# A matmul queue that no longer waits on its own semaphore, one moved matmul pair and a reordered load queue in a fused attention and gMLP kernel

## The chip, the cores and the metric

The kernel runs on one core of a Trainium2 chip. The metric is device time of one launch in microseconds (us). Traces come from one profiled execution; the times beside them come from separate runs.

## What is computed

The input x is 2048 x 512 in bf16. It is layer-normalised once; two branches read the result, and the output is x plus both. Cut to what matters:

```python
xn = _layernorm(x, axis=-1)
return x + _A_ref(xn, A_wqkv, A_wo) + _B_ref(xn, B_w_in, B_w_sp, B_b_sp, B_w_out)

# _A_ref: H = 32 heads of Dh = 16, each position looks at W = 8 positions, dil = 2 apart
logits = jnp.einsum('bhsd,bhswd->bhsw', q, kg) * scale    # masked where the position is < 0
o = jnp.einsum('bhsw,bhswd->bhsd', _softmax(logits), vg)  # then @ wo

# _B_ref: Fh = 896
z = _gelu(jnp.einsum('bsd,df->bsf', x, w_in))
z1, z2 = z[..., :Fh], _layernorm(z[..., Fh:], axis=-1)
g = jnp.einsum('ts,bsf->btf', w_sp, z2) + b_sp[None, :, None]
return jnp.einsum('bsf,fd->bsd', z1 * g, w_out)
```

## The kernel before

The 2048 positions are cut into 16 blocks of 128 rows, and these into four groups of four. Everything is a list of named tasks; each belongs to one engine, and knows what it reads and writes. `schedule` puts the tasks of each engine in order by estimated times, but `plan.orders` (lines 1037 to 1101) gives long hand-written orders that it must keep. `emit` (line 222) then writes each engine's tasks with the semaphore waits that their dependencies need. Each engine has one semaphore, which every task that isn't a DMA raises by one at its end (`sem_pe` for TensorE); each DMA channel has its own.

In `emit`, a task that depends on an earlier task of the same engine waits for that engine's own semaphore too, unless the engine is already known to have passed it (lines 260 to 277). On TensorE this concerns two tasks that write to the same PSUM bank with nothing of another engine between them.

The names that matter, with their lines:

- `ldx0` to `ldx15` (L543): loads of x blocks, 128 KB each. `ldw_in2a_0`, `ldw_in2b_1` and so on (L553): halves of the z2 part of w_in. `ldq`, `ldk` (L565) and `ldwv` (L573): the q, k and v weights, 512 KB each. SyncE issues most of these; ScalarE's queue issues three of the first ones.
- `bnst`, `bnag` (L610, L613), `rstd` on POOL (L615) and `norm` (L624): the layer norm of one block; `ctr` (L619) is the centring of block 0 alone.
- `xTr0b`, `xTr1a` (L640): transposing a half of a block on TensorE against the identity, two 128x128 matmuls each. `xTe0b`, `xTe1a` (L646): ScalarE's copy of it to SBUF. Only blocks 0 to 3 go this way; `xTd0` and `xTd4` to `xTd15` (L628) are transposes by DMA, issued by SyncE. Block 0 has both: TensorE's copy feeds its z2, `xTd0` feeds the rest.
- `z2_1_0a` (L802): for block 1, output half 0 (448 of the 896 columns) and contraction half a: two 128x448 matmuls. Halves a and b of one output add up in one PSUM bank. For block 0 half b comes first. `z2g1_0` (L813): ScalarE's gelu of it, with the sum along the row. `z2s` (L835): the sum of squares.
- `Q0_0`, `K0_0` (L678): q and k for the first group of four blocks, four 128x512 matmuls each. Q0_0 needs the four transposed blocks and `ldq`, K0_0 also `ldk`. `QKe` (L686) copies them out. `V0` (L660) likewise, with `Ve` (L664).
- `prod`, `padd` (L702, L707), `dd`, `sm`, `sz`, `srec`, `sattn` (L727 to L779): DVE's products, sums and softmax.
- `z1` (L825, gelu at L830), then `g0_0` and so on (L935): the product with w_sp, 16 matmuls a task. ScalarE first writes the bias into the bank (`gs`, L929), TensorE adds, and DVE multiplies with z1 (`u`, L942), which frees the bank.
- `out` (L1001, L1005): both output projections into one bank; `fin` (L1014) copies it, `st` (L1017) stores. `OTd` (L973) are the DMA transposes of the attention result that `out` reads.

Before the first loads have landed, TensorE runs eight `warm` matmuls (L582), and one more, `fill0`, between its first transposes and the first z2 half.

TensorE's order begins warm, xTr0b, xTr0a, fill0, z2_0_0b, z2_0_1b, xTr1a, xTr1b, z2_0_0a, z2_0_1a, z2_1_0a, z2_1_0b, z2_1_1a, xTr2a, xTr2b, z2_1_1b, z2_2_0a, z2_2_0b, xTr3a, xTr3b, z2_2_1a, z2_2_1b, z2_3_0a, z2_3_0b, z2_3_1a, z2_3_1b, Q0_0, K0_0. All later TensorE work follows in a fixed order as well: Q, K, V and z2 by groups, z1, g, out.

In the built program ten TensorE tasks wait on `sem_pe`: fill0, z2_0_0a, z2_0_1a, z2_1_0b, z2_1_1b, z2_2_0b, z2_2_1b, z2_3_0b, z2_3_1b and z2_4_0.

Of the kernel before, what the change touches and what calls it, by code (L numbers as in the profile page):

```python
# [14 lines left out]
class Plan:  # L15
# [79 lines left out]
    def schedule(self, lookahead=1000, slack=120.0, dma_bw=300.0, xbar_bw=190.0,  # L95
# [21 lines left out]
        def lat(d, t):  # L117
            if d.dma is not None:
                return 150.0
            if d.eng == t.eng:  # L120
                return 35.0
            return 210.0 if d.eng == "pe" else 80.0

        cur_tbl = [None]
# [10 lines left out]
        while remaining:  # L135
            best = None
            for e in ENGS:
# [6 lines left out]
                for t in pl:  # L144
                    ok = all(p.start is not None for p in before.get(t, ()))
                    ready = 0.0
                    for d in t.deps:
                        if d.end is None:
                            ok = False
                            break  # L150
                        r = d.end + lat(d, t)
                        if r > ready:
                            ready = r
                    if ok:
                        st_ = max(eng_free[e], ready + t.margin)
                        if t.tbl is not None and t.tbl != cur_tbl[0] and cur_tbl[0] is not None:
                            st_ += sw_bias
                        cands.append((st_, t))
# [24 lines left out]
            st, t = best  # L183
            e = t.eng
# [37 lines left out]
    def emit(self, nc, block, sems, chan_sems):  # L222
        cnt = {e: 0 for e in ENGS}
        ccnt = {}
        for e in ENGS:
            for t in self.order[e]:
                if t.dma is None:
                    cnt[e] += 1
                    t.count = cnt[e]
                    t.tok = (("E", e), t.count)  # L230
        for t in self.tasks:
            if t.dma is not None:
                c = t.dma["chan"]
                ccnt[c] = ccnt.get(c, 0) + 16
                t.count = ccnt[c]
                t.tok = (("C", c), t.count)
        self.chan_totals = dict(ccnt)
        for t in sorted(self.tasks, key=lambda x: (x.start, x.idx)):
            ck = {}
            for d in t.deps:  # L240
                for k, v in d.clock.items():
                    if ck.get(k, 0) < v:
                        ck[k] = v
            ck[t.tok[0]] = max(ck.get(t.tok[0], 0), t.tok[1])
            t.clock = ck

        engines = {"pe": nc.tensor, "act": nc.scalar, "dve": nc.vector, "pool": nc.gpsimd, "sp": nc.sync}
        starters = {"pe": block.tensor, "act": block.scalar, "dve": block.vector, "pool": block.gpsimd,
                    "sp": block.sync}
        self.n_waits = 0  # L250

        def semof(key):
            return sems[key[1]] if key[0] == "E" else chan_sems[key[1]]

        def run_engine(e):
            def body(eng):
                known = {}
                for t in self.order[e]:
                    need = {}
                    dl = [d for d in t.deps if known.get(d.tok[0], 0) < d.tok[1]]  # L260
                    for d in dl:
                        k, v = d.tok
                        implied = False
                        for d2 in dl:
                            if d2 is d:
                                continue
                            c2 = d2.clock.get(k, 0)
                            if c2 > v or (c2 == v and d2.tok != d.tok):
                                implied = True
                                break  # L270
                        if implied:
                            continue
                        if need.get(k, 0) < v:
                            need[k] = v
                    for k, v in need.items():
                        eng.wait_ge(semof(k), v)
                        self.n_waits += 1
                    for d in t.deps:
                        for k, v in d.clock.items():
                            if known.get(k, 0) < v:  # L280
                                known[k] = v
                    last = t.fn(eng)
                    assert last is not None, "task %s returned no instruction" % t.name
                    if t.dma is None:
                        last.then_inc(sems[e], 1)
                    else:
                        last.then_inc(chan_sems[t.dma["chan"]], 16)
                self._final_hook(e, eng)
            starters[e](body)

        for e in ENGS:
            run_engine(e)
# [21 lines left out]
    warm=8,  # L314
    fill0=1,
# [4 lines left out]
def build_kernel(nc, A_x, A_wqkv, A_wo, B_x, B_w_in, B_w_sp, B_b_sp, B_w_out, out, report=False, sched_kw=None,  # L320
# [79 lines left out]
    with ExitStack() as es:  # L400
# [633 lines left out]
        for q in qord:  # L1034
# [8 lines left out]
                z2g1_1  # L1043
            """.split(),
            """
                ldx0 ldx1 ldw_in2a_0 ldw_in2b_0 ldx3 ldx4 ldq xTd0 ldx5 ldk ldx6 ldx7 ldwv
            """.split(),
            """
                warm xTr0b xTr0a fill0 z2_0_0b z2_0_1b xTr1a xTr1b z2_0_0a z2_0_1a z2_1_0a z2_1_0b z2_1_1a xTr2a xTr2b
                z2_1_1b z2_2_0a z2_2_0b xTr3a xTr3b z2_2_1a z2_2_1b z2_3_0a z2_3_0b z2_3_1a z2_3_1b Q0_0 K0_0 Q0_1 K0_1  # L1050
                Q0_2 K0_2 Q0_3 K0_3 V0 V1 V2 V3 V4 V5 V6 V7 Q1_0 K1_0 Q1_1 K1_1 Q1_2 K1_2 Q1_3 K1_3 z2_4_0 z2_4_1 z2_5_0
                z2_5_1 z2_6_0 z2_6_1 z2_7_0 z2_7_1 V8 V9 V10 V11 Q2_0 K2_0 Q2_1 K2_1 Q2_2 K2_2 Q2_3 K2_3 z2_8_0 z2_8_1
# [28 lines left out]
                zm0_2 zm2 zq2 sm1_0 sm2_0 sm3_0 ssub0 prod1_2 prod1_3 padd1_1 ze2 zv2 padd1_2 zn8 zn9 zn10 zn11 prod2_0  # L1081
                prod2_1 zm0_3 zm3 zq3 padd2_0 dd0_1 dd1_1 sm1_1 sm2_1 sm3_1 ssub1 ze3 zv3 prod2_2 zn12 zn13 zn14 zn15
                prod2_3 padd2_1 padd2_2 prod3_0 prod3_1 padd3_0 u0_0 prod3_2 u1_0 sz1_0 sz2_0 sz3_0 srec0 sattn0 u2_0
                sz1_1 sz2_1 sz3_1 srec1 sattn1 u3_0 dd0_2 dd1_2 u4_0 sm1_2 sm2_2 sm3_2 ssub2 prod3_3 u5_0 sz1_2 sz2_2
                sz3_2 srec2 u6_0 sattn2 padd3_1 u0_1 padd3_2 u1_1 pv0_0_0 pv0_0_1 u2_1 pva2048_0_0 u3_1 pva1024_0_0
                pvc0_0 u4_1 pv0_1_0 u5_1 dd0_3 dd1_3 sm1_3 u6_1 sm2_3 sm3_3 ssub3 pv0_1_1 u0_2 sz1_3 sz2_3 sz3_3 srec3
                u1_2 sattn3 pva2048_0_1 pva1024_0_1 pvc0_1 pv1_0_0 pv1_0_1 u2_2 pva2048_1_0 u3_2 pva1024_1_0 pvc1_0 u4_2
                pv1_1_0 u5_2 pv1_1_1 pva2048_1_1 pva1024_1_1 pvc1_1 pv2_0_0 u6_2 pv2_0_1 pva2048_2_0 pva1024_2_0 pvc2_0
# [32 lines left out]
def bass_parallel_sum__sliding_local_dilated__mixer_gmlp__prompt_kernel(  # L1121
    nc, A_x, A_wqkv, A_wo, B_x, B_w_in, B_w_sp, B_b_sp, B_w_out, out
):
    build_kernel(nc, A_x, A_wqkv, A_wo, B_x, B_w_in, B_w_sp, B_b_sp, B_w_out, out)
# [28 lines left out]
```

## Time and profile before

| what | value |
|---|---|
| three runs | 237.16 us median, 236.94 to 238.07 |
| the profiled execution | 237.23 us, span 235.1 us |
| TensorE matmuls (PE) | 230.5 us busy, 98% of the span, 1103 instructions |
| VectorE (DVE) | 202.4 us, 86% |
| ScalarE (ACT) | 118.5 us, 50% |
| GpSimd (POOL) | 51.5 us, 22% |
| granted TensorE clock | 1.000 |
| DMA | 41.88 MB, mean 178 GB/s |

The span runs from the first to the last instruction in the trace; the execution's own time is 2.1 us longer. Busy shares are means over stages with different limits, so they don't say what a local change is worth. Matmuls overlap: a 128x448 matmul lasts 352 ns, but in a stream the next one starts 189 ns after it (32 of them in 6.05 us), so a busy TensorE need not be at its pace. PEld is the load of the stationary operand, which goes on beside the matmuls.

### The profile page before, as it was taken

The page shows a single profiled execution, that of the slowest core. Times are in us where ns is not written, and L with a number is a line of the kernel's source. Part 1 is how long each engine was busy: PE and PEld are TensorE (multiplying, and loading weights), DVE is VectorE, ACT ScalarE, POOL GpSimd, SP SyncE. Part 2 cuts the span into 40 slices and gives each one's busy share as a digit, 9 for nine tenths or more (in the row PEclk, how much of TensorE's full clock was granted, in tenths as well). Part 3 has the DMA queues.
Part 4 walks back from the last instruction along what each step waited for, and adds up shares of the span by engine and source line. Part 5 has one row for each costly group of instructions (what it writes and reads, how often), then busy time and mean ns, then how long its engine had stood idle before and what let it go on. Part 6 is the DMA issues. An engine that isn't in the chain of part 4 may idle for free.

```text
span 235.1 us, 2969 instructions
## 1 busy us (share of the span) xinstructions
PE 230.5 (98%) x1103; PEld 109.8 (47%) x1103; DVE 202.4 (86%) x231; ACT 118.5 (50%) x233; POOL 51.5 (22%) x67
## 2 busy tenths in 40 slices
PE   7899999999999999999999999999999999999996
PEld 2344455455454444444444444444444444444454
DVE  4579869998998989997999994999999999999600
ACT  3698578988988987954012125232223432201442
POOL 4437982862591050001201000010000000000000
PEclk9999999999999999999999999999999999999999
DMA  7997670299919799591529999999746788602232
GB/s 230 237 297 140 154 185 16 80 192 283 382 74 174 163 247 284 111 251 46 161 62 256 191 255 256 245 186 354 217 122 174 187 240 216 189 3 45 72 84 67
DMA packets 87709, 41.88 MB, mean 178 GB/s; under 512 B 66816, under 2 KB 86544, under 8 KB 87696
## 3 DMA queue, kind: packets, MB, share of 16 engines
q1 hardware_dynamic: 71616, 23.37, 47.9%
q10 hardware_dynamic: 14640, 14.13, 19.6%
q0 software_dynamic: 1440, 4.21, 6.1%
q8 instruction: 8, 0.13, 0.2%
q14 instruction: 5, 0.04, 0.1%
HBM read 20.05 MB, written 5.26 MB: 108 GB/s over the span
## 4 chain that ended last, share of the span: by engine, by line
PE 96%; DVE 1%; DMA 1%; issue 0%; POOL 0%; ACT 0%
PE ps L935 41%; PE ps L678 12%; PE ps L802 10%; PE ps L1005 10%; PE ps L825 10%; PE ps L1001 6%; PE ps L660 6%; DMA arena<-in_A_x_dram 1%; DVE fpool L610 1%; PE ps L640 0%; POOL fpool L615 0%; DVE arena L619 0%; DVE arena L624 0%; DVE fpool L613 0%; ACT arena L1014 0%
## 5 line engine op out<-in xcount | busy, mean ns | idle before, releaser
L935 PE MATMUL ps<-arena 128*128 128x512 bf16 x448 | 97.5, 379 | 0.0
L935 PEld LDWEIGHTS ps<-arena 128*128 128x128 bf16 x448 | 43.8, 98 | 52.8
L929 ACT ACTIVATE ps<-arena 128x512 f32<-128x512 bf16 x28 | 16.5, 599 | 58.5 <-DVE arena L942 58.4
L960 DVE TENSOR_TENSOR arena<-arena 128x4096 bf16<-128x4096 bf16 x16 | 36.3, 2284 | 0.4
L702 DVE TENSOR_TENSOR arena<-arena 128x4096 bf16<-128x4096 bf16 x16 | 36.1, 2281 | 0.1
L678 PE MATMUL ps<-arena 128*128 128x512 bf16 x128 | 28.3, 379 | 0.0
L964 DVE TENSOR_TENSOR arena<-arena 128x4096 bf16<-128x4096 bf16 (+1 forms) x16 | 28.0, 1752 | 0.3
L707 DVE TENSOR_TENSOR arena<-arena 128x4096 bf16<-128x4096 bf16 x12 | 27.4, 2287 | 0.2
L1005 PE MATMUL ps<-arena 128*128 128x512 bf16 (+2 forms) x126 | 27.1, 355 | 0.0
L802 PE MATMUL ps<-arena 128*128 128x448 bf16 x128 | 26.4, 353 | 0.8 <-ACT arena L646 0.3
L825 PE MATMUL ps<-arena 128*128 128x512 bf16 x112 | 24.3, 379 | 0.0
L678 PEld LDWEIGHTS ps<-arena 128*128 128x128 bf16 x128 | 14.5, 113 | 13.1
L1014 ACT ACTIVATE arena<-ps 128x512 bf16<-128x512 f32 (+2 forms) x17 | 9.5, 557 | 20.0 <-PE ps L1005 18.6
L942 DVE TENSOR_TENSOR arena<-ps,arena 128x512 bf16<-128x512 f32 x28 | 19.0, 679 | 0.0
L1005 PEld LDWEIGHTS ps<-arena 128*128 128x128 bf16 x126 | 13.5, 113 | 11.0
L802 PEld LDWEIGHTS ps<-arena 128*128 128x128 bf16 x128 | 11.8, 98 | 13.6 <-PE ps L802 1.5
L686 ACT ACTIVATE arena<-ps 128x1024 bf16<-128x1024 f32 x16 | 16.3, 1019 | 2.8 <-PE ps L678 2.2
L830 ACT ACTIVATE arena<-ps 128x512 bf16<-128x512 f32 x28 | 16.0, 595 | 3.2 <-PE ps L825 2.7
L813 ACT ACTIVATE arena<-ps 128x448 bf16<-128x448 f32 x30 | 16.2, 544 | 2.6 <-PE ps L802 0.4
L825 PEld LDWEIGHTS ps<-arena 128*128 128x128 bf16 x112 | 11.0, 98 | 13.1
L1001 PE MATMUL ps<-arena 128*128 128x512 bf16 (+2 forms) x72 | 16.8, 355 | 0.0
L835 ACT ACTIVATE arena<-arena 128x896 bf16<-128x896 bf16 x16 | 15.1, 943 | 0.1
(62 smaller groups left out, 191.2 us busy)
## 6 DMA issues: line engine op xcount, KB each, us to landing
arena<-vscr ACTq DMA_DIRECT2D x8, 1152.0 KB, 8.5
arena<-in_A_x_dram ACTq DMA_DIRECT2D x17, 128.0 KB, 5.4
vscr<-arena POOLq DMA_DIRECT2D x16, 128.0 KB, 2.4
arena<-in_A_x_dram SPq DMA_DIRECT2D x15, 128.0 KB, 3.6
out_dram<-arena ACTq DMA_DIRECT2D x15, 128.0 KB, 1.8
arena<-in_A_wqkv_dram SPq DMA_DIRECT2D x3, 512.0 KB, 5.3
ascr<-arena POOLq DMA_DIRECT2D x4, 256.0 KB, 4.7
arena<-ascr POOLq DMA_DIRECT2D x4, 256.0 KB, 3.1
```

The costliest lines, as they stand in the source:

```text
L678: last = t.matmul(bank(k + which), AC(off["wqk"] + 1024 * dc + col0, [[4, 128]]), AC(off["xnT"] + dc * S + 512 * j, [[1, 512]]), start=(dc ...
L702: T("dve", lambda v: v.tensor_tensor(pbv, qb, kb, ALU.mult), reads=[("QT", c, j), ("KT", c, j), ("KTpad", c, j)], writes=[("pb", s_)], est ...
L707: T("dve", lambda v: v.tensor_tensor(A("pb", 4096, 4096 * a), A("pb", 4096, 4096 * a), A("pb", 4096, 4096 * b), ALU.add), reads=[("pb", b) ...
L802: last = t.matmul(ps[:, 512 * k: 512 * k + HF], st, AC(off["w_in"] + 1792 * dc + c0, [[1, HF]]), start=(h == first and dc == 2 * h), stop= ...
L825: lastm = t.matmul(bank(k), AC(off["w_in"] + 1792 * dc + 128 * fc, [[1, 128]]), AC(off["xnT"] + dc * S + 512 * j, [[1, 512]]), start=(dc = ...
L929: T("act", lambda a: a.activation(bank(k), A("bbc", 512, 512 * tc), ACTF.Copy), reads=["bbc"], writes=[("ps", k)], est=c_act(512), name="g ...
L935: last = t.matmul(bank(k), AC(off["z2"] + FH * sh + 128 * fc, [[1, 128]]), AC(off["wT"] + WSL * r_ + sh * 512, [[1, 512]]), start=False, s ...
L942: T("dve", lambda v: v.tensor_tensor(uv, bank(k), uv, ALU.mult), reads=[("ps", k)], writes=[("z1T", fc, tc)], est=c_dve(512) + 20, name="u ...
L960: T("dve", (lambda iv, tv, av: lambda v: v.tensor_tensor(tv, iv, av, ALU.mult))(iv, tv, av), reads=[("attn", j), ("Ve", par)], writes=[("V ...
L964: T("dve", (lambda n: lambda v: v.tensor_tensor(AC(off["Vs"], [[4096, 2], [1, n]]), AC(off["Vs"], [[4096, 2], [1, n]]), AC(off["Vs"] + n, ...
L1001: t.matmul(po, AC(off["OT"] + 512 * ot_pos(tb) + 128 * cc, [[1, 128]]), AC(off["wo"] + 512 * cc + c0, [[1, n]]), start=False, stop=False, ...
L1005: last = t.matmul(po, AC(off["z1T"] + fc * S + t0, [[ts, 128]]), AC(off["w_out"] + 512 * fc + c0, [[1, n]]), start=False, stop=(fc == FC - ...
```

## The change

Four edits, and a shift of all later lines by two:

1. In `emit`, TensorE's tasks no longer wait for TensorE's own semaphore, and what those earlier tasks have waited for is not gone through again. All ten waits on `sem_pe` go; the other engines keep theirs.
2. In TensorE's order z2_0_0a goes from behind xTr1b to in front of xTr1a.
3. In SyncE's order, ldx4, ldq, xTd0, ldx5, ldk becomes ldx4, ldx5, ldq, ldk, xTd0.
4. In the planner a dependency of TensorE on itself counts 0 ns in place of 35. In the built program this and the hand order move, apart from the above, one DVE task: u6_0 stands in front of sz2_2, sz3_2 and srec2 instead of behind them. ScalarE and GpSimd keep their order.

```diff
             if d.eng == t.eng:
-                return 35.0
+                return 0.0 if t.eng == "pe" else 35.0
...
-                    dl = [d for d in t.deps if known.get(d.tok[0], 0) < d.tok[1]]
+                    dl = [d for d in t.deps if known.get(d.tok[0], 0) < d.tok[1] and not (d.eng == e == "pe")]
...
                     for d in t.deps:
+                        if d.eng == e == "pe":
+                            continue
                         for k, v in d.clock.items():
...
-                ldx0 ldx1 ldw_in2a_0 ldw_in2b_0 ldx3 ldx4 ldq xTd0 ldx5 ldk ldx6 ldx7 ldwv
+                ldx0 ldx1 ldw_in2a_0 ldw_in2b_0 ldx3 ldx4 ldx5 ldq ldk xTd0 ldx6 ldx7 ldwv
...
-                warm xTr0b xTr0a fill0 z2_0_0b z2_0_1b xTr1a xTr1b z2_0_0a z2_0_1a z2_1_0a z2_1_0b z2_1_1a xTr2a xTr2b
+                warm xTr0b xTr0a fill0 z2_0_0b z2_0_1b z2_0_0a xTr1a xTr1b z2_0_1a z2_1_0a z2_1_0b z2_1_1a xTr2a xTr2b
...
-                sz1_1 sz2_1 sz3_1 srec1 sattn1 u3_0 dd0_2 dd1_2 u4_0 sm1_2 sm2_2 sm3_2 ssub2 prod3_3 u5_0 sz1_2 sz2_2
-                sz3_2 srec2 u6_0 sattn2 padd3_1 u0_1 padd3_2 u1_1 pv0_0_0 pv0_0_1 u2_1 pva2048_0_0 u3_1 pva1024_0_0
+                sz1_1 sz2_1 sz3_1 srec1 sattn1 u3_0 dd0_2 dd1_2 u4_0 sm1_2 sm2_2 sm3_2 ssub2 prod3_3 u5_0 sz1_2 u6_0
+                sz2_2 sz3_2 srec2 sattn2 padd3_1 u0_1 padd3_2 u1_1 pv0_0_0 pv0_0_1 u2_1 pva2048_0_0 u3_1 pva1024_0_0
```

## The prediction

> **What bounds the kernel now.** I read the page's chain first, then busy time by stage, then the chain in order of time in the one stage that is not full. The page's chain, by engine:
>
> ```profile
> PE 96%; DVE 1%; DMA 1%; issue 0%; POOL 0%; ACT 0%
> ```
>
> So only TensorE's own time counts. Cutting the span where TensorE's work changes gives (first columns: stretch, its length, TensorE's busy time):
>
> ```profile
> 4.60:6.93 2.33, 1.68 (x13) 0.82 (x14) 1.84 (x6) 0.66 (x2) 0.93 (x2) 1.00 0.95 305
> 6.93:14.16 7.23, 6.75 (x40) 2.73 (x37) 4.15 (x12) 5.87 (x20) 2.90 (x6) 1.00 0.97 277
> 14.16:232.87 218.71, 218.67 (x1047) 105.13 (x1045) 194.65 (x209) 110.17 (x209) 45.77 (x50) 1.00 0.74 175
> 232.87:235.10 2.23, 0.00 (x0) 0.00 (x0) 0.00 (x0) 0.27 (x1) 0.00 (x0) 1.00 0.20 51
> ```
>
> From 14.16 us, the first matmul of Q0_0, TensorE is full for 218.7 us. If nothing later becomes late, every us that Q0_0 starts earlier comes off the end. All that the change can win lies before 14.16. The chain in order of time there (start, length, what):
>
> ```profile
> 6.22 0.42 DVE arena L624
> 6.65 0.05 issue
> 6.70 0.40 PE ps L640 x4
> 7.09 1.15 PE ps L802 x6
> 8.24 0.05 issue
> 8.29 0.93 PE ps L802 x4
> 9.22 0.22 PE ps L640 x4
> 9.45 0.93 PE ps L802 x4
> 10.37 0.14 issue
> 10.51 0.54 PE ps L802 x2
> 11.05 0.22 PE ps L640 x4
> 11.27 0.39 PE ps L802 x2
> 11.66 0.05 issue
> 11.71 0.94 PE ps L802 x4
> 12.65 0.14 issue
> ```
>
> TensorE looks busy, but the "issue" pieces of 0.05 and 0.14 us stand where a matmul waited for the full end of the one before. In a stream, 32 L802 matmuls take 6.05 us (chain, 35.04): 0.189 each, although one lasts 0.352. From 6.93 to 14.16 there are 28 of them and 8 transposing ones (0.055 apart): 28 x 0.189 + 8 x 0.055 = 5.73 of 7.23 us. **1.50 us are stalls.**
>
> **Part 1, own waits gone.** Single starts, from TensorE's timeline in narrow windows: z2_1_0b starts 0.414 behind the matmul before it (7.877 to 8.291) where the stream has 0.189: 0.226 lost. z2_2_1b (11.711) and z2_3_1b (13.769) lose 0.225 each. z2_2_0b (10.511) and z2_3_0b (12.791) wait for two semaphores and lose 0.315 and 0.314. Sum 1.305. The own waits of fill0, z2_0_0a, z2_0_1a and z2_1_1b cost nothing now (spacing 0.055 at the last). Could hardware need the pause? Inside each half two matmuls add to the same bank 0.189 apart, so no. Bounds: 0 to 1.305; I take 1.305, nearest to that row. At the double waits ScalarE had released long before (10.04 for 10.51, 11.86 for 12.79).
>
> A rule against so much: the Trainium skill, "TensorE: Matmul & The Clock Gate", gives under "Single matmul latency" and "Back-to-back issue gap" (398+N)/2.4 and N/2.4+2.5 ns; for N=448 a drained matmul then costs 163 ns more, five of them 0.82 us. The trace's 0.225 to 0.315 has the semaphore's way in it; by the page the gain would be 0.49 us smaller.
>
> **Part 2, z2_0_0a moved.** After z2_0_1b's second matmul (6.001) TensorE is free at 6.19 and waits for xTr1, which DVE's norm1 releases (6.22 + 0.42, start 6.697). z2_0_0a is ready: xTe0a ended at 5.57, its weights landed at 5.36. Its two matmuls fill 6.19 to 6.57: 0.377 off the stretch, xTr1 not delayed. Bounds 0 to 0.377; I take 0.377.
>
> **What is late next.** Replaying the new order by the rows: xTr1 at 6.70, z2_0_1a at 6.93 and 7.12, then z2_1_0a could start at 7.31, but its copy xTe1a ends at 7.40 (ScalarE L646, 7.02, pair of 0.66): it starts at 7.46, 0.15 late. xTr2 is due at 8.59, norm2 ends at 8.55 (8.13 + 0.41): 0.02. z2_2_0a is due at 9.22, but ScalarE does two gelus (L813) until 8.91 and then xTe2a, 0.38: 9.37, 0.15 late (0.14 now). xTr3 due 10.12, norm3 ended at 9.79. xTe3a: ScalarE free at 10.22, xTr3 done at about 10.40, copy until 10.82, z2_3_0a due at 11.10. After it nothing stops: z2_3_1b at 12.23, **Q0_0 at 12.60 instead of 14.16: 1.56 us**. Check: 1.305 + 0.377 + 0.139 (the old copy wait) + 0.057 (rest) - 0.32 (the new stalls) = 1.56. Without the new stalls 1.88.
>
> **Part 3, SP's queue.** SyncE's rows now:
>
> ```profile
> 5.76 0.43 SPq L565 DMA_DIRECT2D arena<-in_A_wqkv_dram  x1
> 6.24 1.30 SPq L628 DMA_TRANSPOSE arena<-arena  x1
> 7.59 0.57 SPq L543 DMA_DIRECT2D arena<-in_A_x_dram  x1
> 8.21 0.42 SPq L565 DMA_DIRECT2D arena<-in_A_wqkv_dram  x1
> ```
>
> q weights, block 0's transpose (xTd0), x block 5, k weights. New: x5 at 5.76, q at about 6.2, k at 6.7, xTd0 at 7.15; x6, x7 and the v weights issue 0.2 earlier than now. K0_0 needs k 0.86 after Q0_0: 13.46 in the new times. Now k lands at about 13.5 (8.21 + 5.3, the longest landing of L565), just when needed; issued 1.5 earlier it is early. x5 ends DVE's 2.11 us wait at 12.00, which is off the path: nothing. The price is xTd0: Q0_0 reads all four blocks, so it waits for it. Now it lands at 10.62 (6.24 + 4.4). The new landing I bound below by its issue, 7.15 + 4.4 = 11.5, and above by what x5 and k took behind it (13.46 - 10.62 = 2.84): 13.46. Between: the DMA moved 58 GB/s from 7 to 8 us and 234 from 10 to 11, against 325 to 350 in full stretches; x5 fills the first hole, the earlier k the second. Estimate: q's data starts at 8.5 (2.3 after issue, as the 7-8 hole shows), 1.1 MB of q and k at 350 GB/s end at 11.5, the transpose 0.6 later as now (10.02, 10.62): **12.1 to 12.2**, with 12.46 as the latest that costs nothing. I take no delay; the bound keeps 0 to 1.0.
>
> The skill's "DMA: Bandwidth & Descriptors" speaks against this part: "Queues, rings and completion order" says that each engine consumes its descriptors in ring order, so the transpose stands behind 640 KB more; at the 358 GB/s of its "Specifications" that is 1.83 us and a landing at 12.45.
>
> **Part 4, cover behind 14.16.** TensorE runs 1.56 earlier; who is not early by itself? From 15.9 us on, what other engines release comes at least 2.5 us ahead of TensorE, mostly 3 to 10, with three exceptions. K1_3 at 34.0 is released at 32.38 (ScalarE L664, 31.77 + 0.60): 1.64, just enough. out3_0 at 188.15 needs a transpose issued at 181.48 and landed 4.7 later: 1.9, enough. g1_1 starts at 125.56 (97.93 + 128 x 0.2158) and its bank preload (ScalarE L929, 124.45 + 0.60) ends at 125.05: 0.5, which would give back 1.06. But the DVE edit puts u6_0 (L942, 123.79) in front of three softmax steps (0.29, 0.29, 0.95): it can start at about 122.2, the preload ends near 123.5, and g1_1 is due at 124.00. Covered even if DVE gains nothing.
>
> **The sum.** The profiled execution took 237.23 us (span 235.1; 0.07 above the median of 237.16). 237.23 - 1.56 = 235.67; I say **235.7**.
>
> **Rivals.** (a) The transpose is late: landing at 13.46, Q0_0 at 13.60, gain 0.56, time 236.7. For it: the k load goes in front, and x5's and k's arrivals behind the transpose were slow. Against: the two holes. (b) A cover fails: u6_0 is late in a DVE whose order moved, or ScalarE in the head; up to 1.06 back: 236.7. Against: 0.5 us of spare at g1_1. (c) The edit doesn't do what it says: TensorE drains between tasks anyway, leaving 0.38 - 0.32: 237.2. Against: the 0.189 spacing. (d) Slower: the transpose shares the engines with the loads behind it and lands with the v weights, 15.75 now; Q0_0 at 15.89, 1.73 late, 239.0. It decides against the change once the landing passes 14.02. For it: between 14 and 16 us the DMA is full; against: now it landed 0.6 behind q with loads waiting.
>
> **How the numbers follow.** Forecast (gain 1.3 to 1.88) 0.62, a 0.20, b 0.10, c 0.04, d 0.04. Low end: all stalls avoided, 237.23 - 1.88 = 235.35, less 0.25 (the fastest run shown lies 0.29 under the profiled one): 235.1. High end: a's 236.7 plus 0.2: 236.9. About 0.5%, 1.19 us, is what a measurement can tell here: a gain of 1.19 needs a landing before 12.83, so the forecast and 0.06 of a and b are faster: 0.68; d 0.04 slower; 0.28 the same.
>
> **What would show it.** Right: L802 starts 0.189 apart within the head, no own waits of TensorE, Q0_0 (L680 after) at 12.6, the stretch to the end still 218.7 us. Part 3 wrong: Q0_0 starting right on the transpose's landing after 12.5. Part 4 wrong: a gap at g1_1, 124 us. Part 1 wrong: spacings of 0.41 that remain.

## The result, and the profile after

The changed kernel takes 236.37 us (median of 20 runs, 235.81 to 237.42) where the kernel before took 237.16 (20 runs beside them): ratio 0.9964, 95% interval 0.9950 to 0.9978, so 0.85 us less (0.79 by the medians). Forecast were 235.7 and 1.56 us. The sign and the range hold; nearly half of the gain is missing, and the gain is below the 0.5% that the prediction called faster. The profiled execution took 236.17 us with a span of 234.0, against 237.23 and 235.1. Of all the runs told of here one, of k_behind (247.75 us), was in a slower state; it enters no figure.

The page's chain by engine, the answer to "PE 96%":

```profile
PE 99%; ACT 0%; issue 0%
```

Busy time by stage (columns: stretch, its length, busy time of PE, PEld, DVE, ACT and POOL, clock, DMA share, GB/s):

```profile
4.43:6.80 2.37, 2.28 (x9) 1.01 (x10) 1.88 (x6) 0.66 (x2) 0.93 (x2) 1.00 0.85 269
6.80:13.09 6.29, 6.29 (x41) 3.26 (x40) 4.49 (x13) 5.26 (x19) 2.92 (x6) 1.00 1.02 301
13.09:231.80 218.71, 218.67 (x1047) 105.15 (x1045) 194.52 (x208) 110.54 (x212) 45.91 (x50) 1.00 0.73 176
231.80:234.00 2.20, 0.00 (x0) 0.00 (x0) 0.00 (x0) 0.28 (x1) 0.00 (x0) 1.00 0.21 52
```

The stretch from Q0_0 to TensorE's end lasts 218.71 us in both kernels: behind Q0_0 nothing was lost and nothing won. Q0_0 starts at 13.09 instead of 14.16, and that is the whole difference. The chain in order of time in the head (start, length, what):

```profile
5.37 1.97 PE ps L804 x6
7.34 0.22 PE ps L642 x4
7.57 1.67 PE ps L804 x8
9.24 0.22 PE ps L642 x4
9.46 1.30 PE ps L804 x6
10.76 0.22 PE ps L642 x4
10.98 2.27 PE ps L804 x12
13.25 2.81 PE ps L680 x13
```

The "issue" pieces are gone, and the twelve L804 matmuls at the end take 2.27 us, 0.189 each. So the stalls did go; yet Q0_0 was forecast at 12.60. What took the 0.49 us stands ahead of this, between 4.4 and 7.2 us.

SyncE's rows after:

```profile
2.63 3.73 SPq L545 DMA_DIRECT2D arena<-in_A_x_dram  x3
6.40 0.98 SPq L567 DMA_DIRECT2D arena<-in_A_wqkv_dram  x2
7.43 1.29 SPq L630 DMA_TRANSPOSE arena<-arena  x1
```

The transpose xTd0 is issued at 7.43, not at 7.15, and lands at 12.41; k lands at 11.89.

**One measure for all runs.** x block 0 lands between 2.72 and 3.30 us in the profiles, which shifts all of an execution (in the profile after 0.16 us sooner than in the one before). I therefore take the time from TensorE's first transposing matmul (first L642, or L640 in unshifted code) to Q0_0, "the head" from here on. Where the trace has lost the first record of Q0_0, its start is worked out: the last group of twelve L804 starts in a stream plus 12 x 0.189, which for the kernel after gives 10.82 + 2.27 = 13.09, as recorded. Before: 14.16 - 4.60 = 9.56. After: 13.09 - 4.43 = 8.66. Forecast: 12.60 - 4.60 = 8.00.

### The profile page after: what moved, and what is told of

Its sections match the earlier page's. It is cut to its first block, busy times and chain, and to the rows that moved or that the text cites. A ratio compares the mean times of both kernels' runs of the same rounds, so it can differ in the third digit from the quotient of the medians.

```text
span 234.0 us, 2964 instructions
## 1 busy us (share of the span) xinstructions
PE 230.8 (99%) x1103; PEld 110.5 (47%) x1103; DVE 202.6 (87%) x231; ACT 118.2 (51%) x233; POOL 51.7 (22%) x67
## 4 chain that ended last, share of the span: by engine, by line
PE 99%; ACT 0%; issue 0%
PE ps L937 41%; PE ps L680 12%; PE ps L804 11%; PE ps L1007 10%; PE ps L827 10%; PE ps L1003 6%; PE ps L662 6%; PE ps L584 2%; PE ps L642 1%; ACT arena L1016 0%
## 5 line engine op out<-in xcount | busy, mean ns | idle before, releaser
L804 PE MATMUL ps<-arena 128*128 128x448 bf16 x128 | 26.4, 359 | 0.1
L944 DVE TENSOR_TENSOR arena<-ps,arena 128x512 bf16<-128x512 f32 x28 | 19.1, 681 | 0.1
L804 PEld LDWEIGHTS ps<-arena 128*128 128x128 bf16 x128 | 12.3, 99 | 12.6 <-issue 1.4
```

The source lines that it names most:

```text
L804: last = t.matmul(ps[:, 512 * k: 512 * k + HF], st, AC(off["w_in"] + 1792 * dc + c0, [[1, HF]]), start=(h == first and dc == 2 * h), stop= ...
L944: T("dve", lambda v: v.tensor_tensor(uv, bank(k), uv, ALU.mult), reads=[("ps", k)], writes=[("z1T", fc, tc)], est=c_dve(512) + 20, name="u ...
```

## The experiments

Three theories stood for the missing part. **G**: TensorE's clock rises at a time of its own in each execution, and a late rise now costs time. **L**: the landing of xTd0 or of the k weights is late. **D**: DVE is late, because of x block 5, and a thin cover fails. All twelve kernels, each compared with runs of the kernel before that were taken beside it:

| kernel | median us (runs) | ratio to before [95%] | span median (range) |
|---|---|---|---|
| waits_only | 236.30 (11) | 0.9937 [0.9916, 0.9957] | 234.2 (233.6-234.3) |
| own_waits_kept | 237.37 (12) | 0.9998 [0.9972, 1.0023] | 234.9 |
| old_loads | 236.01 (7) | 0.9936 [0.9910, 0.9963] | 233.9 (233.5-234.3) |
| old_u6 | 236.62 (12) | 0.9966 [0.9945, 0.9986] | 234.35 (233.8-234.8) |
| k_behind | 236.58 (11) | 0.9964 [0.9936, 0.9993] | 233.9 (233.5-235.7) |
| k_behind_no_move | 236.44 (12) | 0.9971 [0.9949, 0.9993] | 234.1 (233.6-235.3) |
| k_behind_cold | 237.03 (12) | 0.9989 [0.9973, 1.0005] | 234.9 (234.3-235.5) |
| before_cold | 238.45 (12) | 1.0045 [1.0027, 1.0063] | 236.3 (235.5-237.0) |
| qq_kk | 236.00 (6) | 0.9945 [0.9930, 0.9960] | 233.9 (233.7-234.2) |
| act_k | 236.04 (6) | 0.9943 [0.9928, 0.9957] | 234.05 (233.8-234.3) |
| act_k_x5 | 236.02 (11) | 0.9958 [0.9942, 0.9974] | 234.1 (233.6-235.4) |
| after_again | 236.43 (12) | 0.9973 [0.9956, 0.9990] | 234.3 (233.8-235.7) |

The kernel before has a span median of 235.0 to 235.1 throughout, the kernel after 234.15 (233.7 to 235.3).

**waits_only**: the kernel before with edit 1 alone.

```diff
-                    dl = [d for d in t.deps if known.get(d.tok[0], 0) < d.tok[1]]
+                    dl = [d for d in t.deps if known.get(d.tok[0], 0) < d.tok[1] and not (d.eng == e == "pe")]
...
+                        if d.eng == e == "pe":
+                            continue
```

> The kernel before with TensorE's own waits gone, everything else as it was (old order, old loads, u6_0 at its old place). Theory G (the changed kernel has no pause left in its head, so an execution whose TensorE clock rises late, as in its profile at 6.8 us, loses 0.5 us there that the kernel before hides in its pause from 6.2 to 6.7): here the pause is still there, so the gain is about the sum of the five stalls, 1.2 to 1.3 us, and the runs lie as close together as those of before. Theory L (in unprofiled runs the transpose of block 0 lands late behind the k weights): no transpose behind k here; K0_0 may wait for k instead (13.46 us), which caps the gain at 1.4. Theory D (something behind the head gives it back; g1_1 has only 0.5 us of spare with u6_0 at its old place): gain 0.5 to 1.0, and a gap of TensorE at g1_1.

TensorE's timeline:

```profile
4.71 0.39 PE L642 MATMUL ps<-arena 128*128 128x128 bf16 x4 [0.37 <-DVE arena L621]
...
6.81 0.40 PE L642 MATMUL ps<-arena 128*128 128x128 bf16 x4 [0.34 <-DVE arena L626]
7.04 2.06 PE L804 MATMUL ps<-arena 128*128 128x448 bf16 x10
...
10.68 2.43 PE L804 MATMUL ps<-arena 128*128 128x448 bf16 x12
```

The ten L804 at 7.04 take 2.06 us, nine steps of 0.189 and one duration: no stall is left among them. Q0_0 at 10.68 + 2.27 = 12.95, head 8.24, 1.32 us shorter than before. Behind it K0_0 waits 0.3 us for k, which lands at 14.05 (K0_0 at 14.10). The median is 1.04 below the 237.34 of the kernel before beside it.

**own_waits_kept**: the kernel after with its own waits back in `emit` (edits 1 and 4's cost undone, both orders kept).

```diff
-                return 0.0 if t.eng == "pe" else 35.0
+                return 35.0
...
-                    dl = [d for d in t.deps if known.get(d.tok[0], 0) < d.tok[1] and not (d.eng == e == "pe")]
+                    dl = [d for d in t.deps if known.get(d.tok[0], 0) < d.tok[1]]
...
-                        if d.eng == e == "pe":
-                            continue
```

> The changed kernel with TensorE's own waits put back, moved pair and loads as changed. By the prediction's rows only the moved pair is left: 0.38 less the new wait for the copy xTe1a 0.15, so 0.2 us faster than before, Q0_0 near 13.9. G: with a late clock the pair costs what it wins: 0 gain, and a wider spread than before. L: no loss, since Q0_0 comes long after 12.4.

The chain in order of time shows the old pattern again:

```profile
11.23 0.05 issue
11.28 0.94 PE ps L802 x4
12.22 0.14 issue
12.36 0.93 PE ps L802 x4
13.29 0.05 issue
13.33 0.55 PE ps L802 x2
```

Q0_0 follows two steps behind 13.33, at 13.71; the head is 13.71 - 4.38 = 9.33, 1.3 us longer than old_loads below. The time can't be told from that of the kernel before (237.37 against 237.34); only the span median is 0.2 us lower (234.9 against 235.1), as expected from the moved pair. So edit 1 carries nearly the whole gain. xTd0 landed at 12.98 here, hidden under the stalls.

**old_loads**: the kernel after with the old load order.

```diff
-                ldx0 ldx1 ldw_in2a_0 ldw_in2b_0 ldx3 ldx4 ldx5 ldq ldk xTd0 ldx6 ldx7 ldwv
+                ldx0 ldx1 ldw_in2a_0 ldw_in2b_0 ldx3 ldx4 ldq xTd0 ldx5 ldk ldx6 ldx7 ldwv
```

> The changed kernel with the old order of the loads (q, transpose of block 0, x block 5, k). The transpose lands at 10.6 again, but k at 13.46. L: Q0_0 is free, K0_0 starts at 13.6: gain up to 1.4 and more than the changed kernel's 0.85. G: the same loss by the clock as in the changed kernel: gain 0.85, give or take 0.2. If the reordering of the loads is worth what the prediction says, a profile with an early clock shows K0_0 waiting for k by some 0.1 us.

Its profile caught an early clock. TensorE's timeline, first of this kernel, then of the kernel after:

```profile
4.40 0.39 PE L642 MATMUL ps<-arena 128*128 128x128 bf16 x4 [0.45 <-DVE arena L621]
4.63 0.30 PE L584 MATMUL ps<-const-bfloat16-1.0 128*128 128x320 bf16 x1
5.24 1.29 PE L804 MATMUL ps<-arena 128*128 128x448 bf16 x6 [0.31 <-ACT arena L648]
6.50 0.40 PE L642 MATMUL ps<-arena 128*128 128x128 bf16 x4
...
10.16 2.43 PE L804 MATMUL ps<-arena 128*128 128x448 bf16 x12
```

```profile
4.43 0.58 PE L642 MATMUL ps<-arena 128*128 128x128 bf16 x4
4.81 0.47 PE L584 MATMUL ps<-const-bfloat16-1.0 128*128 128x320 bf16 x1
5.37 1.97 PE L804 MATMUL ps<-arena 128*128 128x448 bf16 x6
7.18 0.39 PE L642 MATMUL ps<-arena 128*128 128x128 bf16 x4
...
10.82 2.43 PE L804 MATMUL ps<-arena 128*128 128x448 bf16 x12
```

The same instructions: 0.39 against 0.58, 0.30 against 0.47, 1.29 against 1.97 us; from 7.18 on the two go at the same pace. In the kernel after TensorE ran at half clock until 6.79 (the trace's clock event); here until 3.43. The next transposes come 2.10 us behind the first ones here and 2.75 there: **0.65 us is the price of the late clock.** The load order isn't what makes this difference: in after_again, the kernel after once more with the rise at 5.45, they come 2.10 behind again (4.47, 6.57). In old_u6, with the rise at 6.62, they come 2.57 behind (4.63, 7.20), 0.47 late. The stages' clock column said 1.00 throughout and doesn't show it; durations do. Head here: 10.16 + 2.27 - 4.40 = 8.03, forecast 8.00. The price of the old order is the wait for k, in the chain of this kernel:

```profile
8.56 4.98 DMA arena<-in_A_wqkv_dram
13.54 0.05 issue
13.59 2.57 PE ps L680 x11
```

K0_0 starts at 13.59 and was due at 12.43 + 0.86 = 13.29. In spite of it the median is 0.36 us below that of the kernel after.

**old_u6**: the kernel after with u6_0 at its old place in DVE's order.

```diff
-                ... prod3_3 u5_0 sz1_2 u6_0
-                sz2_2 sz3_2 srec2 sattn2
+                ... prod3_3 u5_0 sz1_2 sz2_2
+                sz3_2 srec2 u6_0 sattn2
```

> The changed kernel with u6_0 behind the three softmax steps again. In the changed kernel's trace DVE moved 1.1 us ahead with TensorE, so u6_0 would end near 124.1 at its old place, the preload near 123.9 to 124.7, and g1_1 is due at 124.5. Prediction: 0 to 0.3 us slower than the changed kernel by a gap at g1_1. D: clearly slower (0.5 to 1.0). G and L: no difference.

g1_1's bank preload, in ScalarE's timeline of this kernel and of the kernel after:

```profile
123.42 0.60 ACT L931 ACTIVATE ps<-arena 128x512 f32<-128x512 bf16 x1 [4.26 <-DVE arena L944]
```

```profile
121.96 0.60 ACT L931 ACTIVATE ps<-arena 128x512 f32<-128x512 bf16 x1 [2.84 <-DVE arena L944]
```

The preload ends at 124.02, 1.46 us later, and TensorE still runs without a gap there. The times can't be told from those of the kernel after. Moving u6_0 bought cover that nobody used, since DVE as a whole has moved a us ahead: before, this preload ended at 125.05. Most of that doesn't come from x block 5: in waits_only, with x block 5 and u6_0 both at their old places, the preload ends at 124.32 (123.72 + 0.60), and TensorE doesn't wait for it either.

**k_behind**: old order, but k directly behind the transpose and x block 5 behind k; the rest as after.

```diff
-                ldx0 ldx1 ldw_in2a_0 ldw_in2b_0 ldx3 ldx4 ldx5 ldq ldk xTd0 ldx6 ldx7 ldwv
+                ldx0 ldx1 ldw_in2a_0 ldw_in2b_0 ldx3 ldx4 ldq xTd0 ldk ldx5 ldx6 ldx7 ldwv
```

> The changed kernel with the loads in the order x block 4, q, transpose of block 0, k, x block 5: the transpose again directly behind q, the k weights directly behind it. Theory L (the transpose behind k lands between 12.4 and 13.0 us, and Q0_0, due at 12.6 with an early clock, waits for it; in the old order k lands at 13.5 to 14.05 and K0_0 waits): here the transpose lands near 10.9 and k near 12.6, so neither waits, Q0_0 starts at 12.6 with an early clock and 13.1 with a late one; spans from 233.4 to 234.0 us, median 233.7, against 234.15 of the changed kernel: 0.2 to 0.5 us faster than it, gain on before 1.2 to 1.5. Theory G alone (the clock explains all that is missing): the same spread and median as the changed kernel, 234.15.

k, issued at 7.92, lands at 13.47, 2.65 us behind the transpose (10.82) and hardly sooner than with x block 5 in front of it (13.54). Where k directly follows q, in the four profiles with the new order, it lands only 1.50 to 1.72 us behind q. So behind the transpose k is slow, with x block 5 between them or without. x block 5 lands at 13.81 instead of 8.06, and the chain now runs through DVE (in order of time, around g1_1):

```profile
122.64 0.60 DVE arena L944
123.24 0.33 DVE arena L769
123.57 0.61 DVE arena L944
124.18 0.02 issue
124.21 0.61 ACT ps L931
124.82 0.05 issue
124.86 1.25 PE ps L937 x5
```

u6_0 (the L944 at 123.57) is 2.3 us later than the 121.24 of the kernel after, and g1_1 waits for the preload. From Q0_0 to TensorE's last weight load 219.78 us pass instead of 218.59: 1.19 us of stalls (K0_0, K1_3 at 32 us, g1_1). Theory D is right where x block 5 comes late; in the kernel after it doesn't.

**k_behind_no_move**: the same, with z2_0_0a behind xTr1b again.

```diff
-                warm xTr0b xTr0a fill0 z2_0_0b z2_0_1b z2_0_0a xTr1a xTr1b z2_0_1a
+                warm xTr0b xTr0a fill0 z2_0_0b z2_0_1b xTr1a xTr1b z2_0_0a z2_0_1a
```

> As k_behind, but with z2_0_0a behind the transposes of block 1 again, as before the change. By the prediction the moved pair is worth 0.38 less the new wait for the copy xTe1a, 0.15: 0.2 us slower than k_behind with an early clock. G: with a late clock the pause hides the slow matmuls, and the two are equal, so 0.1 to 0.2 slower in the median, and spans closer together than those of k_behind.

From the first transposes to Q0_0 it takes 0.10 us longer than k_behind (by weight loads, 8.08 against 7.98), and nothing is lost behind Q0_0 (218.61), since Q0_0 is 0.4 us later there and x block 5 landed 0.27 sooner. 236.44 and 236.58 can't be told apart. In k_behind the first pair behind the transposes of block 1 waited 0.27 us for its half of w_in (landed at 6.69), which took part of what the move won. The move is worth little or nothing where a late DVE takes it back.

**k_behind_cold, before_cold**: only two warm matmuls instead of eight, so that the clock is late in every execution.

```diff
-    warm=8,
+    warm=2,
```

> As k_behind, but with two warm matmuls in place of eight, so that TensorE idles from 1.6 to 4.4 us and its clock must rise later. G: L804 matmuls 0.373 apart until the rise, somewhere between 7.5 and 11 us; each one costs 0.185 us, so 1 to 3 us slower than k_behind. If slow matmuls cost nothing (L alone): no change, since nothing but the warm matmuls is left out, whose results are read by nobody.

> The kernel before with two warm matmuls in place of eight. G: slower than before too, but by less than k_behind_cold is slower than k_behind (about 0.5 us less), because its pauses hide part of the slow matmuls: some 0.5 to 2.5 us.

The clock rose at 9.6 us in before_cold, and by the durations at about 8.9 in k_behind_cold. Span medians rise by 1.3 us in the kernel before (235.0 to 236.3) and by 1.0 in k_behind (233.9 to 234.9). That a late clock costs time is plain; that it costs the kernel before less was wrong for a rise this late. The heads lost about the same (by weight loads 9.40 to 11.03, and 7.98 to 9.49). k_behind got part of it back: with Q0_0 1.6 us later no stall is left behind it (218.59).

**qq_kk**: old_loads with Q0_1 in front of K0_0, so that k has 0.86 us more.

```diff
-                z2_3_1b Q0_0 K0_0 Q0_1 K0_1
+                z2_3_1b Q0_0 Q0_1 K0_0 K0_1
```

> The kernel after with its old load order (q weights, transpose of block 0, x block 5, k weights) and Q0_1 set in front of K0_0. With the old load order the transpose was early (10.92 us in the earlier profile) and the k weights late (13.54, K0_0 waited for them 0.2 to 0.5 us). Theory L (landings set the rest of the loss): Q0_1 takes the 0.86 us in which K0_0 waited, K0_0 is due only 1.73 us behind Q0_0, at about 14.3, and nothing waits: no gap at K0_0, Q0_0 to the end 218.6 instead of 218.9, span median 233.6 instead of 233.9, time 235.7. Theory G (clock rise alone): the spread between executions comes from the rise of TensorE's clock, so the median stays within 0.1 us of the old load order (236.0) and only its late executions differ. Third theory: Q0_0 and Q0_1 need the transpose and the q weights alone, so if x block 5 is what is late (DVE), the order of Q and K changes nothing: 236.0 and gaps at K0_0's new place.

No wait at K0_0 (k landed at 13.92), 218.59 us behind Q0_0, and the head is 10.46 + 2.27 - 4.70 = 8.03 again. Still the time is 236.00, as old_loads. The step was right in the profile and is not seen in the median: x block 0 landed 0.30 us later in this profile than in that of old_loads, and such shifts between executions are as large as the 0.3 us sought.

**act_k and act_k_x5**: old_loads with k issued by ScalarE behind its copy xTe0a; in the second one x block 5 in front of q as well.

```diff
-        for which, eng in ((0, "sp"), (1, "sp")):
+        for which, eng in ((0, "sp"), (1, "act")):
...
-                actprime ldw_in2a_1 ldw_in2b_1 ldx2 xTe0b xTe0a xTe1a
+                actprime ldw_in2a_1 ldw_in2b_1 ldx2 xTe0b xTe0a ldk xTe1a
...
-                ldx0 ldx1 ldw_in2a_0 ldw_in2b_0 ldx3 ldx4 ldq xTd0 ldx5 ldk ldx6 ldx7 ldwv
+                ldx0 ldx1 ldw_in2a_0 ldw_in2b_0 ldx3 ldx4 ldq xTd0 ldx5 ldx6 ldx7 ldwv
```

> The kernel after with the k weights issued from ScalarE's queue behind its copy xTe0a (about 5.8 us, where ScalarE idles until 6.8), SyncE's queue in the order x4, q weights, transpose, x5. Theory R (a load behind the transpose in the same queue starts late): k lands before 12, though it shares the engines with q, and the transpose near 11.5, before its due time of 12.46; Q0_0 waits for neither, K0_0 neither; span 233.4 to 233.9 by the clock's rise, time near 235.7. Theory B (the bytes in front decide, not the queue): the transpose waits for q and k all the same and lands near 12.2 to 12.4 as in the kernel after, x5 behind it near 13.5, DVE late, a gap at 32 us and at g1_1: time 236.4 or more. ScalarE's issue costs it 0.4 us of idle; if its copy xTe1a starts later than 6.9 with an early clock, that is the price.

> As the run with k weights on ScalarE's queue, but x block 5 in front of the q weights on SyncE's, so that DVE is early whatever the transpose does. Theory R: k before 12, transpose 0.4 us later than in that run, near 12, x5 near 8; no gap at 32 us or at g1_1; span 233.4 to 233.9, time 235.7. Theory B: the transpose at 12.4 or later, Q0_0 starting right on its landing as in the kernel after with own waits kept (12.98): time 236.2 to 236.5, no better than the kernel after.

k lands at 10.45, as theory R said, but the transpose at 12.50, as theory B said: it pays for k's bytes from another queue too, since q, in front of it, landed at 11.91 instead of 10.32. Neither Q0_0 nor K0_0 waited for a load (218.59 behind Q0_0). Yet the head took 8.51, 0.48 more than in old_loads: two pairs of z2 matmuls waited 0.21 and 0.25 us for halves of w_in, which landed at 5.72 and 6.96 (in old_loads at 5.20 and 6.46). 236.04 is no better than old_loads. With x block 5 in front as well the profiled execution was one of the late ones (span 235.4). x block 4 landed at 10.61 instead of near 7.6. DVE's statistics of block 4 stand in front of norm3 in its order, so the transposes of block 3 came late (TensorE's timeline):

```profile
11.70 0.40 PE L642 MATMUL ps<-arena 128*128 128x128 bf16 x4 [1.23 <-DVE arena L626]
```

The transpose xTd0 landed at 14.29 in it, and Q0_0, due at 14.20, waited another 0.2 us for it.

**after_again**: the changed kernel once more, unedited.

> The changed kernel itself once more, for a second profile and more spans: its 20 spans run from 233.7 to 235.3, 8 of them at 234.5 or more, and one profile can't say what the late ones waited for. Theory L: x block 0's transpose lands at 12.4 or later in about half the executions, so this profile shows either Q0_0 starting within 0.2 us of the landing, or a landing within 0.3 us ahead of it, and the spans again reach past 234.5, as those of the old load order (at most 234.3) don't. Theory G: the clock rises anywhere between 3.4 and 6.8 us, the transpose is in time, and only a rise past 6.2 us costs anything (up to 0.5 us), so no span is above 234.3 by it. Measured from x block 0's landing to Q0_0 the head takes 9.3 us where neither holds (old load order: 9.26), 9.7 to 9.9 with a late rise, more than 10 with a late transpose. Span median 234.1, time 236.3.

The chain in order of time:

```profile
7.84 5.37 DMA arena<-arena
13.21 0.14 issue
13.35 2.75 PE ps L680 x12
```

Here the clock rose at 5.45 and cost nothing: TensorE's last twelve z2 matmuls start at 10.23, so Q0_0 was due at 12.50. It starts at 13.35, 0.14 behind the landing of the transpose: **0.85 us lost to xTd0.** Over both runs of this kernel 10 of 32 spans are at 234.5 or above (15 of 44 with old_u6, which has the same load order). With the old order (waits_only, old_loads, qq_kk) none of 24 is; the largest is 234.3.

## Why the prediction was right in sign and short in size

**Part 1 was right.** Forecast 1.305 us from the five stalls; the head shrank by 1.32 with edit 1 alone and lost the gain when the waits came back. The measured price of such a wait stands. The Trainium skill's "TensorE: Matmul & The Clock Gate", whose "Single matmul latency" and "Back-to-back issue gap" were weighed in the prediction, makes the five 0.82 us; the runs side with the rows.

**Part 2, and what is late next, were right.** The prediction booked 0.377 + 0.139 + 0.057 - 0.32 = 0.25 us for them together; waits_only and old_loads differ by 8.24 - 8.03 = 0.21, k_behind and k_behind_no_move by 0.10. The whole replay (8.00 for the head) holds to 0.03 in old_loads and qq_kk, whose clock costs nothing and whose xTd0 is in time. In k_behind and act_k it is 0.1 to 0.5 us short: there TensorE also waited for halves of w_in, whose landing the prediction took as fixed. Rival c (nothing happens) is refuted.

**"I take no delay" in part 3 failed.** The estimate was a landing at 12.1 to 12.2. In the four profiles with the new order xTd0 landed at 12.41, 12.65, 12.98 and 13.21. One term was the issue of xTd0: "x5 at 5.76, q at about 6.2" took the landing of w_in2a, for which x blocks 4 and 5 wait, as fixed at 5.36. It was 5.37 to 5.94, so xTd0 was issued at 7.28 to 7.84 instead of 7.15 (0.13 late even in the earliest). The other term was the way behind q and k, 4.98 to 5.50 us against the 5.0 assumed. This is rival a, at 0 to 0.85 us. The Trainium skill's "DMA: Bandwidth & Descriptors", "Queues, rings and completion order", from which the prediction worked out 12.45, was nearer; all four landings but one lie above that too.

**The clock was missing from the prediction.** It took the pace of before's profile, where the rise came at 3.79. In the ten traces with eight warm matmuls that record it, it lies between 3.43 and 6.79; a rise at 5.55 (qq_kk) cost nothing, one at 6.62 (old_u6) 0.47 and one at 6.79 0.65 us. The Trainium skill's "TensorE: Matmul & The Clock Gate", "What's actually happening", says that the gate watches a window of 3413 ns that runs freely and isn't reset by the kernel. The spread of 3.36 us agrees with a window of that length, and not with the ±500 ns that the section gives for the variation; the earliest rise came 2.7 us after the first warm matmul (0.77), sooner than a full window of work.

So the profile after adds up: 12.60, less 0.17 for an earlier start, plus 0.65 for the clock, is 13.08 (13.09 measured).

**"k ... issued 1.5 earlier is early" was right** (11.89 to 12.71, never waited for). **"x5 ... off the path: nothing" was right too.** In old_loads x block 5 lands at 11.63 instead of 8.06, and TensorE loses nothing behind K0_0. What the prediction didn't ask is how late it may come: at 13.81 (k_behind) DVE is late, and of the 1.19 us lost there all but K0_0's 0.38 falls on K1_3 and g1_1.

**Part 4 was right** in its result: no gap behind Q0_0 (218.71). But u6_0's move wasn't what covered g1_1. Rival b happened in k_behind only; rival d nowhere.

**The range held by the room left for rivals.** The gain of 0.85 us lies below the 1.3 to 1.88 of the forecast itself; 236.9 as the high end was there for rival a, and the clock, which took 0.65 us in the profiled execution, was no part of it. To that extent the hit is luck.

**Balance of the load edit.** It trades a wait of K0_0 for k, 0.3 us in both old-order profiles that have edit 1 and K0_0 next to Q0_0, for one of Q0_0 for xTd0, 0 to 0.85. The medians (236.01 without the edit, 236.37 and 236.43 with it) and the spans lean against it; the ratios' intervals overlap, so this is likely, not settled.

**What stays open.** How often each loss occurs can't be counted, as only profiled executions show it. The fastest spans of every version with edit 1 and eight warm matmuls (233.5 to 233.8) come to within 0.3 us of the forecast's 233.54. No version tried beats old_loads clearly: old_loads, qq_kk, act_k and act_k_x5 lie within 0.04 us of each other. That an early clock alone would bring the median to the forecast wasn't tried, since TensorE's warm matmuls already start as soon as the program lets them. That the kernel before hides a late rise of this size in its pause at 6.2 to 6.7 us is not shown either: the two profiles of its matmul order that record a rise behind eight warm matmuls have it at 3.79 and 4.39 (before, waits_only).

## What to carry to other kernels

Price a same-engine wait by the stream: spacing at the wait minus spacing without it, taken from the narrow timeline; here that gave the size to 0.02 us. Before moving a load in front of another, take the spread of what its issue waits for and of its landing, not one profile's value, and ask whose cover the displaced load was: a slack of 0.3 us is no slack when landings spread by 0.8. Once stalls are removed from a start-up, a late clock may cost time that idle time hid before, so look at the durations of the first matmuls before a trace is used as a price list.

## What the runs showed of the hardware

- TensorE's clock rose between 3.43 and 6.79 us in executions with the same eight warm matmuls, and at 9.6 (before_cold) and about 8.9 (k_behind_cold) with two. Until then a 128x448 matmul lasted 577 ns and came 373 ns behind the one before it, instead of 352 and 189. The profile's clock column shows 1.00 in these stretches.
- A wait of a 128x448 matmul on the end of the one before it costs 0.225 us, with a second semaphore in the same wait 0.315 (kernel before).
- A 512 KB load directly behind the transpose in its queue landed 2.65 us behind it (k at 13.47 in k_behind); directly behind q, a load as large as itself, it landed 1.50 to 1.72 us behind that (kernel after, after_again, old_u6, own_waits_kept). Moving k up by one place behind the transpose (8.56 to 7.92 us of issue) gained 0.07 us.
- A load on another queue delayed the transpose about as much as one in its own: xTd0 landed at 12.50 in act_k, 12.41 in the kernel after, 10.92 in old_loads.
